# The last 512-column matmul of each second-product run, done as two matmuls of 256 columns

## The chip, the cores and the metric

The kernel runs on one core of a Trainium2 chip. The metric is the device time of one launch in microseconds, as the median of several runs. Five engines work side by side in a core: TensorE (PE in the rows; its weight loads are listed apart as PEld), VectorE (DVE), ScalarE (ACT), GpSimd (POOL) and SyncE (SP), which issues the DMAs.

## The reference

Three layers follow one another: attention with a memory term, a mixture of eight experts over 2304 tokens, and a two-matrix layer.

```python
def _moe_ref(x, w_gate, w1, w2):
    ...
    for e in range(E):
        h = np.maximum(x @ w1[e], 0.0)
        ye = h @ w2[e]
        out += P[:, e:e + 1] * ye

def _moe2_ref(x, w_in, w_out):
    h = x @ w_in
    g = np.maximum(0.01 * h, h)
    return g @ w_out
```

Tokens 2304, model width 512, eight experts of width 1024, then one layer of width 2048. All in float32; the kernel splits each operand into a high and a low part and multiplies three times (high by high, high by low, low by high).

## The kernel before

Attention and the first expert take the first fifth of the span. Everything after that is the main stage, the function `rest`: experts 1 to 7 and the last layer. Its order is written out by hand (manual scheduling); what stands in the code is what each engine does, in that order.

The main stage is a list of steps. A step is one block of tokens by 256 columns of the hidden width. There are four segments (line 749): 14 units by three token blocks, 14 by two, 4 by three, 4 by two, each times two halves (`fp`), which makes 84 + 56 + 24 + 16 = 180 steps. Blocks 0 and 1 of a segment have 512 tokens, block 2 has 256; so 144 steps have 512 tokens and 36 have 256.

A step has two products on TensorE:

- `l1` (line 781), the first product. For 512 tokens it is seven products (`PRODUCTS`, a Strassen-like scheme) of six matmuls each: 42 matmuls of 256 columns, all at line 810. For 256 tokens it is 24 matmuls of 256 columns, at line 798. The operands come in threes: weights high with x high, weights high with x low, weights low with x high.
- `l2` (line 841), the second product, into the PSUM banks `po[j]`, one for each 128 tokens. It is a run of 24 matmuls (12 for 256 tokens) of 512 columns, all at line 853: over two halves `f`, over `j`, and three operand pairs (`hh` with the high weights, `hh` with the low ones, `hl` with the high ones). Here a part of the hidden values (`hh`, `hl`) is the stationary operand, and the 512 columns of the second weight matrix stream through.

The loop of `rest` does `l1` of step k, and then `l2` of step k-1 (lines 962 and 965). So on TensorE a run of 42 or 24 matmuls of 256 columns and a run of 24 or 12 matmuls of 512 columns take turns, with two exceptions at the ends: two `l1` stand ahead of the first `l2`, and two `l2` stand at the end. In nine places eight transposes of 128 columns (line 915, which bring in the tokens of the next layer) stand between an `l2` and the next `l1`. Every matmul has its own weight load of 128 columns.

After the second half of a step (`fp` = 1), VectorE adds each `po[j]` to the accumulator `acc` (lines 861 to 867).

Of the kernel before, what the change touches and what calls it, by code (L numbers as in the profile page):

```python
# [20 lines left out]
P = 128  # L21
B, H, S, D = 4, 8, 576, 64
NT, DM, E, F, G = 2304, 512, 8, 1024, 2048
# [477 lines left out]
class First:  # L501
# [3 lines left out]
    T = 256  # L505
# [63 lines left out]
SB = 256  # L569
# [168 lines left out]
def rest(tc, pools, W, X, xd, Pm, ident, keep, out, conv):  # L738
# [3 lines left out]
    nc = tc.nc  # L742
# [16 lines left out]
    po, hs = {}, {}  # L759

    def tiles(st):

        seg, s = st[0], st[2]
        T = SB if s == 2 else 2 * SB
        return T, range(4 * s, 4 * s + T // P), seg["bases"][0] // P
# [75 lines left out]
    def l2(st):  # L841
        seg, u, s, fp, inst = st
        w = W.finish(inst)
        hh, hl = hs.pop(st[1:])
        T, ts, t0 = tiles(st)
        if fp == 0:
            for j in range(T // P):
                po[j] = pp.tile([P, DM], F32, tag=f"po{j}", name=f"po{j}")
        for f in range(2):
            for j in range(T // P):  # L850
                r = slice(j * P, (j + 1) * P)
                for n, (a, part) in enumerate(((hh, "h"), (hh, "l"), (hl, "h"))):
                    nc.tensor.matmul(po[j], a[:, f, r], w[1, part][:, f], start=(fp == 0 and f == 0 and n == 0), stop=(fp == 1 and f == 1 and n == 2))  # L853
        if last_of[inst] is st:
            W.gone.add((inst, 1))
        if fp == 0:
            return
        e = u // 2
        for j, t in enumerate(ts):
            if u == 2:  # L860
                nc.vector.tensor_scalar(out=acc[t], in0=acc[t], scalar1=Pm[:, t0 + t, 0:1], scalar2=None, op0=ALU.mult)
            if u < 16:
                nc.vector.scalar_tensor_tensor(out=acc[t], in0=po[j], scalar=Pm[:, t0 + t, e:e + 1], in1=acc[t], op0=ALU.mult, op1=ALU.add)  # L863
            elif u == 16:
                nc.scalar.activation(acc[t], po[j], AF.Copy)  # L865
            else:
                nc.vector.tensor_add(acc[t], po[j], acc[t])
            if u == 19:
                nc.sync.dma_start(out=out[(t0 + t) * P:(t0 + t + 1) * P, :], in_=acc[t])
# [84 lines left out]
    for k, st in enumerate(steps):  # L954
        seg, u, s, fp, inst = st
        if more is None or seg is not steps[k - 1][0]:
            assert more is None or next(more, None) is None
            more = side(seg["n"])
        for t in put_by:
            nc.sync.dma_start(out=keep[t * P:(t + 1) * P, :], in_=acc[t - seg_t0])  # L960
        put_by = []
        l1(st)
        if k:
            last = steps[k - 1]
            l2(last)
            if last[1] == 15 and last[3] == 1:
                _, ts, seg_t0 = tiles(last)
                put_by = [seg_t0 + t for t in ts]
        W.advance()
        next(more, None)  # L970
        if seg["n"] < 2:
            conv.advance(1 + (k % 2 if seg["n"] == 0 else 1))
    l2(steps[-1])
    assert next(more, None) is None and next(conv.todo, None) is None

# [174 lines left out]
```

## Time and profile before

| what | us |
|---|---|
| median of 3 runs | 2171.53 |
| lowest and highest | 2171.14, 2173.83 |
| the profiled execution, its own time | 2172.86 |
| the profiled execution, span from first to last instruction | 2171.1 |
| TensorE busy in the span | 2127.4 |
| VectorE busy in the span | 1384.9 |

The span is the time between the first and the last instruction of the profiled execution; 1.8 us of its own time lie around it. A matmul's busy time in the rows is longer than the distance to the next matmul, because matmuls overlap in the pipeline: what a matmul costs is read from the starts of neighbours in the timeline.

### The profile page before, as it was taken

What the parts mean: (1) busy time and instruction counts of PE and PEld (TensorE: products, weight loads), DVE (VectorE), ACT (ScalarE), POOL (GpSimd) and SP (SyncE); (2) the same over time, 40 slices, a digit from 0 to 9 for tenths busy, and PEclk for the clock granted to TensorE, in tenths of its full rate; (3) what the DMA queues carried; (4) which work ended last, traced back from release to release, by engine and by line L of the source; (5) the groups of instructions that cost most, each with busy time, mean ns of one, the idle gap of its engine ahead of it and who ended that gap; (6) DMA issues with size and microseconds to landing.
All of it is one profiled execution on the core that took longest, in us unless ns stands there. A gap on an engine that the chain in (4) does not pass through costs nothing.

```text
span 2171.1 us, 34909 instructions
## 1 busy us (share of the span) xinstructions
PE 2127.4 (98%) x13661; PEld 1878.7 (87%) x13661; DVE 1384.9 (64%) x2523; ACT 758.3 (35%) x1557; POOL 1082.2 (50%) x1007
## 2 busy tenths in 40 slices
PE   7999999999999999999999999999999999999999
PEld 4677777898899999999999889999999998898998
DVE  6666655367767777777766889655545453566565
ACT  6666652333322222222222233333232323333331
POOL 5322223447755544455445688745554444574540
PEclk8999999999999999999999999999999999999999
DMA  7433312245422221122226444311111152336111
GB/s 223 125 121 122 122 59 69 97 144 165 139 69 69 69 68 58 64 69 76 71 72 242 133 143 141 101 59 40 59 49 50 59 213 80 96 91 239 58 50 40
DMA packets 164582, 217.82 MB, mean 100 GB/s; under 512 B 14145, under 2 KB 109377, under 8 KB 162881
## 3 DMA queue, kind: packets, MB, share of 16 engines
q1 hardware_dynamic: 164416, 215.59, 30.5%
q8 instruction: 108, 1.77, 0.3%
q14 instruction: 58, 0.47, 0.1%
HBM read 166.23 MB, written 49.28 MB: 99 GB/s over the span
## 4 chain that ended last, share of the span: by engine, by line
PE 68%; DVE 5%; POOL 4%; issue 2%; DMA 2%; ACT 1%; POOLq 0%; DVEq 0%; SPq 0%; ACTq 0%
PE po L853 35%; PE pq L810 28%; PE pq L798 4%; PE po L493 1%; PE ph L485 1%; POOL w0l L600 1%; DMA raw<-in_moe_w_dram 1%; DVE hl L829 1%; POOL stl L658 1%; DMA xa<-xd 1%; POOL ql L600 0%; DVE c L820 0%; DVE c L831 0%; DVE acc L863 0%; POOL raw L614 0%
## 5 line engine op out<-in xcount | busy, mean ns | idle before, releaser
L853 PE MATMUL po<-w,hh 128*128 128x512 f32 x2592 | 799.0, 389 | 6.8 <-ACT acc L865 2.9
L853 PEld LDWEIGHTS po<-w,hh 128*128 128x128 f32 x2592 | 473.9, 188 | 95.9 <-ACT acc L865 3.1
L853 PE MATMUL po<-w,hl 128*128 128x512 f32 x1296 | 504.4, 389 | 0.0
L600 POOL TENSOR_TENSOR w0l<-raw,w0h 128x512 fp32r<-128x512 f32 x144 | 190.5, 1343 | 364.6 <-ACT w0h L599 364.6
L828 ACT ACTIVATE hh<-c 128x512 fp32r<-128x512 f32 x224 | 129.2, 624 | 482.3 <-DVE c L823 482.3
L853 PEld LDWEIGHTS po<-w,hl 128*128 128x128 f32 x1296 | 243.2, 188 | 50.7
L810 PE MATMUL pq<-Xh,w0h 128*128 128x256 f32 x960 | 270.8, 282 | 3.6 <-ACT xa L928 2.2
L810 PE MATMUL pq<-Xh,w0l 128*128 128x256 f32 x960 | 270.3, 282 | 0.0
L810 PE MATMUL pq<-Xl,w0h 128*128 128x256 f32 x960 | 270.3, 282 | 0.0
L829 DVE SCALAR_TENSOR_TENSOR hl<-c,hh 128x512 fp32r<-128x512 f32 x224 | 165.5, 780 | 79.1 <-ACT hh L828 79.1
L863 DVE SCALAR_TENSOR_TENSOR acc<-po,Pm,acc 128x512 f32<-128x512 f32 x252 | 176.0, 748 | 50.6 <-PE po L853 48.7
L600 POOL TENSOR_TENSOR w<-raw,w 128x512 fp32r<-128x512 f32 x144 | 197.6, 1390 | 0.9
L810 PEld LDWEIGHTS pq<-Xh,w0h 128*128 128x128 f32 x960 | 180.8, 188 | 8.0 <-ACT xa L928 2.4
L810 PEld LDWEIGHTS pq<-Xh,w0l 128*128 128x128 f32 x960 | 184.8, 192 | 0.0
L810 PEld LDWEIGHTS pq<-Xl,w0h 128*128 128x128 f32 x960 | 180.8, 188 | 3.5
L818 DVE TENSOR_TENSOR uv<-pq,s 128x256 f32<-128x256 f32 x144 | 60.4, 419 | 193.3 <-ACT s L817 193.2
L817 ACT ACTIVATE s<-pq 128x256 f32<-128x256 f32 x144 | 54.7, 380 | 257.9 <-PE pq L810 257.8
L600 POOL TENSOR_TENSOR ql<-raw,qh 128x512 fp32r<-128x512 f32 x48 | 62.6, 1325 | 134.1 <-ACT qh L599 134.1
L810 PE MATMUL pq<-Xh,w1h 128*128 128x256 f32 x384 | 107.9, 281 | 1.1 <-ACT xa L928 1.1
L810 PE MATMUL pq<-Xh,w1l 128*128 128x256 f32 x384 | 107.8, 281 | 0.0
L810 PE MATMUL pq<-Xl,w1h 128*128 128x256 f32 x384 | 107.8, 281 | 0.0
L810 PE MATMUL pq<-Xl,sh 128*128 128x256 f32 x384 | 107.8, 281 | 0.0
(257 smaller groups left out, 4847.1 us busy)
## 6 DMA issues: line engine op xcount, KB each, us to landing
raw<-in_moe_w_dram SPq DMA_DIRECT2D x136, 512.0 KB, 3.5
Xh<-kh SPq DMA_DIRECT2D x6, 1792.0 KB, 7.3
Xl<-kl SPq DMA_DIRECT2D x6, 1792.0 KB, 11.5
f<-in_moe_w_in_dram SPq DMA_DIRECT2D x16, 512.0 KB, 5.0
f<-in_moe_w_out_dram SPq DMA_DIRECT2D x16, 512.0 KB, 4.5
raw<-wide_in SPq DMA_DIRECT2D x16, 512.0 KB, 3.2
raw<-wide_out SPq DMA_DIRECT2D x16, 512.0 KB, 3.8
kh<-sth SPq DMA_DIRECT2D x12, 512.0 KB, 5.1
```

What stands on the lines that cost most here:

```text
L485: nc.tensor.matmul(ph[:, :T], wp[:, c, f0:f0 + P], x[:, c, t0:t0 + T], start=(n == 0), stop=(n == 11))
L493: nc.tensor.matmul(po, a[:, s], wp[:, c, :], start=(first and n == 0), stop=(last and n == 2))
L600: self.nc.gpsimd.tensor_sub(lo, src, f32(hi))
L658: sub(lo[:, m], r, f32(hi[:, m]))
L798: nc.tensor.matmul(ph[:, f * SB:(f + 1) * SB], wp(a, c % 2), xp[x][:, c], start=(n == 0), stop=(n == 11))
L810: nc.tensor.matmul(b[-1][:, o:o + SB], wp(a, c), X[s][part][:, x, c], start=(n == 0), stop=(n == 5))
L817: nc.scalar.activation(s1, b[0][:, lo], AF.Copy)
L818: v.tensor_add(uv[:, 0], b[0][:, up], s1)
L828: nc.scalar.activation(hh[:, f], c, AF.Relu)
L829: v.scalar_tensor_tensor(out=hl[:, f], in0=c, scalar=0.0, in1=f32(hh[:, f]), op0=ALU.max, op1=ALU.subtract)
L853: nc.tensor.matmul(po[j], a[:, f, r], w[1, part][:, f], start=(fp == 0 and f == 0 and n == 0), stop=(fp == 1 and f == 1 and n == 2))
L863: nc.vector.scalar_tensor_tensor(out=acc[t], in0=po[j], scalar=Pm[:, t0 + t, e:e + 1], in1=acc[t], op0=ALU.mult, op1=ALU.add)
```

## The change

In each `l2`, the very last matmul of the run (second half `f`, last token tile `j`, third operand pair: `hl` with the high weights) is written as two matmuls, one over columns 0 to 255 and one over columns 256 to 511 of the same bank, with the same stationary operand. The flag that ends the accumulation goes to the second of them. Nothing else is changed.

```diff
                 for n, (a, part) in enumerate(((hh, "h"), (hh, "l"), (hl, "h"))):
-                    nc.tensor.matmul(po[j], a[:, f, r], w[1, part][:, f], start=(fp == 0 and f == 0 and n == 0), stop=(fp == 1 and f == 1 and n == 2))
+                    for d in (slice(0, SB), slice(SB, DM)) if f and n == 2 and j == T // P - 1 else (slice(0, DM),):
+                        nc.tensor.matmul(po[j][:, d], a[:, f, r], w[1, part][:, f, d], start=(fp == 0 and f == 0 and n == 0), stop=(fp == 1 and f == 1 and n == 2 and d.stop == DM))
```

The order on TensorE where an `l2` ends and the next `l1` begins, before (`po_4884` is the bank of the last token tile, `x2` two alike):

```order
L853 MATMUL po_4884<-w_4234,hh 128x512 x2
L853 MATMUL po_4884<-w_4234,hl 128x512
L810 MATMUL pq<-Xh_3477,qh_3480 128x256
L810 MATMUL pq<-Xl_3478,qh_3480 128x256
L810 MATMUL pq<-Xh_3477,ql_3481 128x256
```

The same place in the changed kernel:

```order
L854 MATMUL po_4884<-w_4234,hh 128x512 x2
L854 MATMUL po_4884<-w_4234,hl 128x256 x2
L810 MATMUL pq<-Xh_3477,qh_3480 128x256
L810 MATMUL pq<-Xl_3478,qh_3480 128x256
L810 MATMUL pq<-Xh_3477,ql_3481 128x256
```

The row of one 512-column matmul has become a row of two with 256 columns, each with a weight load of its own; the unbroken chain of 256-column matmuls that follows is now 44 long (26 for 256 tokens) where it was 42 (24). No wait is added on any engine, and the other engines keep their order.

## Rows read from the trace of the kernel before

**Rows 1.** The page: span; busy times; line 853's group (count, busy us, mean ns, idle).

```profile
span 2171.1 us, 34909 instructions
PE 2127.4 (98%) x13661; PEld 1878.7 (87%) x13661; DVE 1384.9 (64%) x2523; ACT 758.3 (35%) x1557; POOL 1082.2 (50%) x1007
...
L853 PE MATMUL po<-w,hh 128*128 128x512 f32 x2592 | 799.0, 389 | 6.8 <-ACT acc L865 2.9
```

**Rows 2.** Two stretches: length, busy time by engine, clock, DMA; columns in first row.

```profile
core 0: us, PE busy (x) PEld busy (x) DVE busy (x) ACT busy (x) POOL busy (x), PEclk, DMA share, GB/s
458.30:463.79 5.49, 5.49 (x27) 4.51 (x25) 2.92 (x5) 3.03 (x6) 5.18 (x7) 1.00 0.05 17
468.74:474.18 5.44, 5.44 (x27) 4.50 (x26) 4.43 (x10) 1.01 (x2) 0.00 (x0) 1.00 0.83 281
```

**Rows 3.** TensorE's waits from 448 us on: total us, times, longest.

```profile
PE pq L810 <- ACT xa L928: 3.3, 2, 2.2
PE po L853 <- ACT acc L865: 2.9, 1, 2.9
PE po L853 <- DVE acc L863: 2.5, 5, 0.9
PE po L853 <- DVE acc L867: 1.3, 1, 1.3
PE pq L810 <- DVE uv L818: 1.2, 1, 1.2
```

**Rows 4.** TensorE's timeline through one step: start, us, engine, line, instruction.

```profile
463.79 0.28 PE L810 MATMUL pq<-Xh,qh 128*128 128x256 f32 x1
...
468.74 0.62 PE L853 MATMUL po<-w,hh 128*128 128x512 f32 x2
...
470.77 0.62 PE L853 MATMUL po<-w,hh 128*128 128x512 f32 x2
...
474.18 0.28 PE L810 MATMUL pq<-Xh,w0h 128*128 128x256 f32 x1
```

**Rows 5.** The same timeline in the first run of the second product.

```profile
458.30 0.63 PE L853 MATMUL po<-w,hh 128*128 128x512 f32 x2
458.77 0.40 PE L853 MATMUL po<-w,hl 128*128 128x512 f32 x1
459.01 0.62 PE L853 MATMUL po<-w,hh 128*128 128x512 f32 x2
...
460.39 0.61 PE L853 MATMUL po<-w,hh 128*128 128x512 f32 x2
```

**Rows 6.** Weight loads, 448.6 to 458.2 us, by operands: count, busy us, mean ns.

```profile
L810 PEld LDWEIGHTS pq<-Xh,w0h 128*128 128x128 f32 x14 | 2.7, 192 | 0.0
L810 PEld LDWEIGHTS pq<-Xh,w0l 128*128 128x128 f32 x14 | 2.6, 188 | 0.0
...
L853 PEld LDWEIGHTS po<-w,hh 128*128 128x128 f32 x1 | 0.2, 192 | 0.0
```

**Rows 7.** Weight loads of the next run, 463.8 to 468.7 us, same columns.

```profile
L810 PEld LDWEIGHTS pq<-Xh,sl 128*128 128x128 f32 x8 | 1.5, 192 | 0.0
...
L853 PEld LDWEIGHTS po<-w,hh 128*128 128x128 f32 x1 | 0.2, 187 | 0.0
```

**Rows 8.** TensorE's timeline in a run of 256 columns that follows transposes.

```profile
1225.05 0.28 PE L810 MATMUL pq<-Xh,qh 128*128 128x256 f32 x1
...
1229.47 0.63 PE L853 MATMUL po<-w,hh 128*128 128x512 f32 x2
...
1230.16 0.62 PE L853 MATMUL po<-w,hh 128*128 128x512 f32 x2
```

**Rows 9.** TensorE's timeline in the stage of the first expert, six matmuls apart.

```profile
442.51 0.39 PE L493 MATMUL po<-w1h,hh 128*128 128x512 f32 x1
...
443.89 0.28 PE L485 MATMUL ph<-xh,w0h 128*128 128x256 f32 x1
```

**Rows 10.** Half of the transposes: count, shortest, median, longest ns, first and last.

```profile
L915 PE MATMUL xt<-ident,ta x36: 272/273/273, 1223.8 to 1929.6; 128*128 128x128 f32 x36
```

## The prediction

> **What bounds the kernel now.** I read the busy shares first: TensorE is busy for 2127.4 of 2171.1 us, the next engine for 1384.9 [rows 1]. The list of TensorE's waits comes next. From 448 us to the end, which is the whole main stage, it waits for another engine some 11 us in all, in ten places [rows 3]. In the other 1700 us one matmul starts as soon as the one ahead of it lets it. The granted clock is 1.00, the upper of its two levels (2.4 GHz), in the stretches I looked at [rows 2]. So whatever the change adds on TensorE in the main stage is added to the end, and what it takes away there comes off; the other engines need not be followed, because they wait for TensorE and not the reverse. No wait is added and no queue is reordered: the second half of the split carries the signal to VectorE that the whole matmul carried.
>
> What is left is the price of one matmul after another, and that is read from starts. In a usual step the 42 matmuls of 256 columns take 468.74 - 463.79 = 4.95 us, 117.8 ns each; the 24 of 512 columns take 474.18 - 468.74 = 5.44 us, 226.7 ns each [rows 4]. Rows print hundredths of a microsecond, and the unrounded starts behind them give the same to a few tenths of a nanosecond.
>
> **Part 1, the split itself.** Two matmuls of 256 columns in place of one of 512 cost 2 x 117.8 - 226.7 = 8.9 ns if each costs what its kind costs in a usual step. There is one per step: 180 x 8.9 ns = 1.6 us. The lower bound for the pair is the cheapest 256-column matmul in the trace. In a run that follows transposes the fourth matmul starts at 1225.05 and the first 512-column one, 39 later, at 1229.47: 113.3 ns each [rows 8]. Two of these are 226.7, so the split would cost nothing. I take 8.9 ns, since the pair follows a run of 512 columns, as the usual 256-column runs do, and no transposes.
>
> The Trainium skill ("TensorE: Matmul & The Clock Gate", section "Back-to-back issue gap") gives the gap between warm matmuls as columns over 2.4 GHz plus 2.5 ns, by which the split would cost 2.5 ns, as an estimate 0.45 us for all 180. The trace differs: 256 columns more cost 108.9 ns, and the part that does not grow with the columns is 8.9 ns.
>
> **Part 2, where the 512-column run is entered.** The matmuls of the usual 256-column run repeat with a period of three. It shows in the weight loads: of each three, two take 188 ns and one 192 ns. In a usual run the long load belongs to the third operand pair (x high with weights low), so that after 42, a multiple of three, the first load of the 512-column run is a short one again, 187 ns [rows 7]. Such a run goes at 226.7 ns from its first matmul on. The 24-long chains of the 256-token steps are a multiple of three too.
>
> One run in the trace is entered elsewhere in this period: the first one, at 458.30. The chain ahead of it began after a wait, and its long load lies on the first operand pair (192 against 188), so that the long load also falls on the first matmul of the 512-column run, 192 ns [rows 6]. That run stumbles. Its first nine matmuls take 460.39 - 458.30 = 2.09 us [rows 5], where the nine of a usual run take 470.77 - 468.74 = 2.03 [rows 4]; the whole run takes 5.49 us against 5.44 [rows 2]. The unrounded starts of the two runs give 5.485 and 5.440, so 45 ns; after ten matmuls it is back at 226.7. DMA is not the reason: its share is 0.05 in the run that stumbles and 0.83 in the one that doesn't [rows 2].
>
> The changed kernel puts two matmuls of 256 columns ahead of the 42. If the period starts with the first 256-column matmul behind a 512-column run, as it does now, the chain is 44 (or 26) long, which leaves a remainder of two. The long load then falls on the third, sixth, ... of the chain, which is the first operand pair of the first product, and again on the first matmul of the 512-column run. That is just the place of the run at 458.30. So each run of the second product that is entered from such a chain should stumble by 45 ns, and since this takes ten matmuls, it fits into the 24 and also into the 11 full ones of a 256-token step; the next chain then starts afresh.
>
> How many are entered so: of 180 runs, the first is unchanged (no split ahead of it), nine stand behind a 256-column run that follows transposes (72 transposes, eight in a place [rows 10]) and keep their own start, and up to seven begin with a wait [rows 3]; that leaves 163. 163 x 45 ns = 7.3 us.
>
> **The sum.** 1.6 + 7.3 = 8.9 us. In the ten places where TensorE waits, the step's own 54 ns are partly hidden: at most 10 x 0.054 = 0.5 us off. I take 8.4 us. From the profiled execution's own time, 2172.86, that makes 2181.3; it lies 1.33 us above the median of the runs, 2171.53, so the median of the changed kernel should be 2179.9 us, 0.39% more. Bounds of the two terms: 0 to 8.9 ns for the split; for the stumble 0 (the usual entry) to 60 ns (the nine-matmul rows at the far end of their rounding); so 0 to 11 us.
>
> **Rivals.** *The entry stays in step.* The run at 458.30 is a single clean case of its kind, and it may be the wait ahead of that chain and not its place in the period that makes it stumble; or the pair, which reads the second weights and not x, does not start the period. Then only the split is paid: 1.5 us, 2173.0 us, no change that can be told. For it speaks that the usual runs show nothing at all, against it that the place of the long load is the one thing that sets the two entries apart. The stage of the first expert shows too that entries can differ without a wait: there six 512-column matmuls take 443.89 - 442.51 = 1.38 us, 20 ns over six usual ones [rows 9].
>
> *The pair puts the chain into the cheap state.* After the transposes the 256-column matmuls go at 113.3 ns for the whole run, with 15 ns or so lost at the entry of the 512-column run (three matmuls in 1230.16 - 1229.47 = 0.69 us where usual ones take 0.68) [rows 8]. If two matmuls of 256 columns from another product did what the transposes do, 135 chains of 42 and 34 of 24 would each win 4.5 ns a matmul: 6486 x 4.5 ns = 29 us, less 169 x 15 ns = 2.5 us, less the 1.6 us of the split: 25 us faster, 2147 us. Against it: the transposes have 128 columns, and behind every 512-column run the trace shows the 117.8 ns state, whichever weights and x follow.
>
> *Part of it.* The entry is off, but by an amount that no row shows (the third place of the period): between 0 and 45 ns, so 2173 to 2180.
>
> The rival on the far side of no change is thus the cheap state; it decides only if the second or third matmul behind the split starts 113 ns after its neighbour rather than 118.
>
> **How the numbers follow.** The forecast has 0.67, the entry in step 0.19, the cheap state 0.08, the partial entry 0.06, half of it above and half below the bound. A measurement of this kernel can tell about 0.2% (4.3 us) from no change. So faster 0.08, same 0.22, slower 0.70. The predicted time is the forecast's, 2179.9. The range leaves out the cheap state and the far ends: from 2172.0, which takes in the entry in step (2173.0 less 1 us of scatter between runs), to 2183.5, the upper bound of 11 us on the median with 1 us of scatter.
>
> **What would show it.** In the changed kernel's profile, 256-column rows at line 854 whose neighbours start 0.12 us apart (right for part 1), and 0.11 if the cheap state holds. The long weight load, 192 ns, on the first operand pair of line 810 instead of the third, and on the first load of line 854's run. The first nine 512-column matmuls of a usual run in 2.09 us, not 2.04, the mean duration of the matmuls at that line some nanoseconds above 389 [rows 1], and a run of 24 (23 full ones and the pair) in 5.49 + 0.01 us. If the long load sits there and the run does not stumble, the step from the period to the stumble is wrong; if the load stays on the third pair, the step from the pair to the period is.

## The result, and the profile after

| | before | after |
|---|---|---|
| median, us | 2172.41 (2171.14 to 2173.83, 4 runs) | 2151.75 (2151.47 to 2154.49, 4 runs) |
| ratio, with its 95% interval | | 0.9908 (0.9896 to 0.992) |
| span of the profiled execution, us | 2171.1 | 2149.7 |

The changed kernel is 0.9% faster, where 0.4% slower was forecast; the time lies outside the range. What came is the rival with a chance of 0.08, the cheap state. The page of the changed kernel (what answers to [rows 1]), with the groups of the two products: line, engine, operation, operands, count, then busy us, mean ns, idle time ahead.

```profile
span 2149.7 us, 35269 instructions
PE 2102.0 (98%) x13841; PEld 1858.8 (86%) x13841; DVE 1387.3 (65%) x2523; ACT 758.2 (35%) x1557; POOL 1082.9 (50%) x1007
...
L854 PE MATMUL po<-w,hh 128*128 128x512 f32 x2592 | 802.4, 391 | 9.3 <-DVE acc L864 4.3
...
L810 PE MATMUL pq<-Xh,w0h 128*128 128x256 f32 x960 | 266.7, 278 | 2.1 <-DVE uv L818 1.4
L810 PE MATMUL pq<-Xl,w0h 128*128 128x256 f32 x960 | 265.8, 277 | 0.0
```

180 matmuls more, as planned, and TensorE still busy to 98%, but 25 us less of it, 21 of them in the main stage. The matmuls of line 810 last 276 to 278 ns on average, where they lasted 281 to 282; those of the 512-column run 391 where they lasted 389. So the main stage's gain lies in the first product, which the diff doesn't touch. The timeline of TensorE in one step (columns as in [rows 4]):

```profile
707.11 0.62 PE L854 MATMUL po<-w,hh 128*128 128x512 f32 x2
707.56 0.40 PE L854 MATMUL po<-w,hl 128*128 128x256 f32 x2
707.80 0.29 PE L810 MATMUL pq<-Xh,w0h 128*128 128x256 f32 x1
707.92 0.28 PE L810 MATMUL pq<-Xl,w0h 128*128 128x256 f32 x1
708.04 0.28 PE L810 MATMUL pq<-Xh,w0l 128*128 128x256 f32 x1
708.15 0.28 PE L810 MATMUL pq<-Xh,w0h 128*128 128x256 f32 x1
708.27 0.28 PE L810 MATMUL pq<-Xl,w0h 128*128 128x256 f32 x1
...
712.58 0.63 PE L854 MATMUL po<-w,hh 128*128 128x512 f32 x2
...
713.27 0.62 PE L854 MATMUL po<-w,hh 128*128 128x512 f32 x2
```

From the fifth matmul of the chain, 708.27, to the first of the 512-column run, 712.58, 38 matmuls take 4.31 us: 113.4 ns each, against 117.8 in [rows 4]. The unrounded starts show the way in: the pair 114 and 119 ns, then 121, 122, 115, 115, and 113.3 from there on. The first three matmuls of the next 512-column run take 713.27 - 712.58 = 0.69 us, the small loss of [rows 8] and not the stumble of [rows 5]. The weight loads of this chain (708.2 to 712.5 us: count, busy us, mean ns) have no long one any more; against [rows 6, 7], all are short, and so is the first load of the 512-column run:

```profile
L810 PEld LDWEIGHTS pq<-Xh,w0h 128*128 128x128 f32 x13 | 2.4, 188 | 0.0
L810 PEld LDWEIGHTS pq<-Xh,w0l 128*128 128x128 f32 x13 | 2.4, 188 | 0.0
L810 PEld LDWEIGHTS pq<-Xl,w0h 128*128 128x128 f32 x13 | 2.4, 188 | 0.0
L854 PEld LDWEIGHTS po<-w,hh 128*128 128x128 f32 x1 | 0.2, 187 | 0.0
```

In the trace of the changed kernel all 169 chains that follow a split run directly are in this state; in the trace before, the 169 chains at the same places were in the other one. (The first two chains have no run ahead of them, and nine stand behind transposes; of these nine, all started in the cheap state before, and seven after: at 1344.38 and 1835.88 us the chain starts at 117.8 ns.)

### The profile page after: what moved, and what is told of

Read it like the earlier page. It is cut to its first block, busy times and chain, and to the rows that moved or that the text cites. A ratio compares the mean times of both kernels' runs of the same rounds, so it can differ in the third digit from the quotient of the medians.

```text
span 2149.7 us, 35269 instructions
## 1 busy us (share of the span) xinstructions
PE 2102.0 (98%) x13841; PEld 1858.8 (86%) x13841; DVE 1387.3 (65%) x2523; ACT 758.2 (35%) x1557; POOL 1082.9 (50%) x1007
## 4 chain that ended last, share of the span: by engine, by line
PE 74%; DVE 4%; POOL 2%; issue 2%; ACT 1%; DMA 0%; DVEq 0%; POOLq 0%; ACTq 0%
PE po L854 38%; PE pq L810 29%; PE pq L798 4%; PE po L493 1%; PE ph L485 1%; DVE hl L829 0%; POOL stl L658 0%; POOL ql L600 0%; DVE c L831 0%; DVE acc L864 0%; DMA raw<-in_moe_w_dram 0%; DVE c L820 0%; POOL w0l L600 0%; PE xt L916 0%; POOL raw L614 0%
## 5 line engine op out<-in xcount | busy, mean ns | idle before, releaser
L854 PE MATMUL po<-w,hl 128*128 128x512 f32 (+1 forms) x1476 | 507.0, 364 | 0.0
L854 PEld LDWEIGHTS po<-w,hl 128*128 128x128 f32 x1476 | 277.2, 188 | 58.5
L828 ACT ACTIVATE hh<-c 128x512 fp32r<-128x512 f32 x224 | 129.2, 624 | 478.2 <-DVE c L823 478.2
L810 PE MATMUL pq<-Xl,w0h 128*128 128x256 f32 x960 | 265.8, 277 | 0.0
L810 PE MATMUL pq<-Xh,w0l 128*128 128x256 f32 x960 | 265.4, 276 | 0.0
L829 DVE SCALAR_TENSOR_TENSOR hl<-c,hh 128x512 fp32r<-128x512 f32 x224 | 170.1, 800 | 79.1 <-ACT hh L828 79.1
L810 PEld LDWEIGHTS pq<-Xh,w0l 128*128 128x128 f32 x960 | 180.4, 188 | 0.0
L832 ACT ACTIVATE hh<-c 128x512 fp32r<-128x512 f32 x64 | 40.5, 632 | 186.6 <-DVE c L831 186.6
L810 PE MATMUL pq<-Xh,sh 128*128 128x256 f32 x384 | 106.2, 277 | 0.0
## 6 DMA issues: line engine op xcount, KB each, us to landing
Xl<-kl SPq DMA_DIRECT2D x6, 1792.0 KB, 11.4
```

The costliest lines, as they stand in the source:

```text
L810: nc.tensor.matmul(b[-1][:, o:o + SB], wp(a, c), X[s][part][:, x, c], start=(n == 0), stop=(n == 5))
L828: nc.scalar.activation(hh[:, f], c, AF.Relu)
L829: v.scalar_tensor_tensor(out=hl[:, f], in0=c, scalar=0.0, in1=f32(hh[:, f]), op0=ALU.max, op1=ALU.subtract)
L832: nc.scalar.activation(hh[:, f], c, AF.Copy)
L854: nc.tensor.matmul(po[j][:, d], a[:, f, r], w[1, part][:, f, d], start=(fp == 0 and f == 0 and n == 0), stop=(fp == 1 and f == 1 and n == ...
```

## The experiments

Words used below: a chain is the run of 42 (or 24) matmuls of the first product; it is cheap at 113.3 ns a matmul and dear at 117.8. The overcost of a step is the time from eleven 512-column matmuls ahead of a chain to ten behind its end, less 226.67 ns for every 512 columns in it, read from the starts in the trace. It takes in the split, the way in, the chain and the entry of the next run. Before, it is 187 ns for a chain of 42 (42 x 4.45); after, 40 ns (5 to 6 for the pair, 20 for the way in, 15 for the entry). Times without an interval are of one run; what is concluded from them rests on the traces, where the overcosts of like steps of one kernel agree within a few ns, and not on the last microsecond.

Theories at the start: N, the neighbour right ahead of the chain sets its state; S, the split acts on the program as a whole (its length, where its pieces lie); A, the addresses that load and stream read together; C, the count.

**Where the split stands, and what it reads: e1 to e4.** e1 splits the last but one matmul of the run, e2 takes the halves in the other order, e3 puts the last but one matmul between them, e4 splits all.

```diff
-todo = [(0, full), (1, full), (2, full)]
+todo = [(0, full), (1, lo), (1, hi), (2, full)] if end else ...     # e1
+todo = [(0, full), (1, full), (2, hi), (2, lo)] if end else ...     # e2
+todo = [(0, full), (2, lo), (1, full), (2, hi)] if end else ...     # e3
+todo = [(n, d) for n in range(3) for d in (lo, hi)]                 # e4
```

> The kernel before, with the last but one matmul of each run of the second product split into two of 256 columns, and the last one left at 512. Theory N (neighbour): what stands right ahead of the first product's chain sets its state; here that is a 512-column matmul again, so the chain goes at 117.8 ns a matmul as before, and the split costs 9 to 30 ns a step: 2172 to 2178 us. Theory S (somewhere): that the run holds a split at all, or that the program is longer by 180 matmuls, is what brings the cheap state: 113.3 ns and about 2152 us.

> The change, with the two halves in the other order (columns 256 to 511 first). If any two 256-column matmuls of the second product ahead of the chain do it (theory N alone): 113.3 ns a matmul in the chain, 2151 to 2153 us. If it hangs on which addresses the pair reads against each other (theory A, addresses): the state can change, 117.8 ns and 2173 to 2181 us.

> The same two halves, but the last but one 512-column matmul stands between them, so that a single 256-column matmul of the second product leads into the chain (43 long, remainder one of three). If the first 256-column matmul behind a 512-column one sets the state by what it reads (theory N): 113.3 ns, 2152 to 2156 us. If it takes two, or a chain of 44 (theory C, count): 117.8 ns and 2173 to 2183 us.

> Every matmul of the second product in the main stage as two of 256 columns, so that the main stage has no 512-column matmul and no change of length. If the cheap state holds wherever it is entered once: two at 113.3 ns cost what one 512-column matmul costs, and the 35 ns or so that each step pays at its two changes of length go: 2143 to 2148 us. If the second product's halves go at 117.8 ns: 24 x 9 ns a step more, about 2186 us, and about 2207 us if the first product's chain goes back to 117.8 ns with it.

Times: e1 2155.88, e2 2153.32, e3 2155.41, e4 2189.33 us, with 2169.9 for the kernel before on the same chip. In all four, all 169 chains are cheap. As e1's chain is 42 long and e3's 43, C falls, and in e2 swapping the halves changes nothing, so nothing there speaks for A. e1 speaks against N: a 512-column matmul stands right ahead of its chain again. But that matmul isn't a usual one: it takes 703.66 - 703.43 = 0.23 us, 233 ns unrounded, where a settled one takes 226.7, and the chain behind it takes a longer way in (117, 117, 118, 122, 118, 114 ns unrounded), which is why e1 is the slower. Timeline of e1:

```profile
703.43 0.40 PE L858 MATMUL po<-w,hl 128*128 128x512 f32 x1
703.66 0.28 PE L798 MATMUL pq<-xph,qh 128*128 128x256 f32 x1
...
704.37 0.28 PE L798 MATMUL pq<-xph,qh 128*128 128x256 f32 x1
704.48 0.28 PE L798 MATMUL pq<-xpl,qh 128*128 128x256 f32 x1
704.59 0.28 PE L798 MATMUL pq<-xph,ql 128*128 128x256 f32 x1
```

e4 lies near the middle number of its expectation, but by other terms: the first product is cheap (276 to 278 ns), while the second product's own 256-column matmuls settle at 120 ns each, worse than either state of the first product. The groups of e4 (count, busy us, mean ns, idle):

```profile
L858 PE MATMUL po<-w,hh 128*128 128x256 f32 x5184 | 831.7, 283 | 5.0 <-ACT acc L870 3.1 <-DVE acc L872 1.2 <-DVE acc L868 0.6
L858 PE MATMUL po<-w,hl 128*128 128x256 f32 x2592 | 522.6, 283 | 0.0
L810 PE MATMUL pq<-Xh,w0h 128*128 128x256 f32 x960 | 266.6, 278 | 1.8 <-DVE uv L818 1.2 <-ACT xa L933 0.5
```

So a fifth theory, P (phase): a settled run of 512-column matmuls hands over in one fixed timing of loads against matmuls, and that timing leads into the dear state; a run disturbed shortly before the handover does not.

**Place, dose, order, size: e5 to e8.**

```diff
-GAPS = {... "X0": 6, "X1": 0, ...}
+GAPS = {... "X0": 4, "X1": 2, ...}                                        # e5
-if f and n == 2 and j == T // P - 1 else
+if s == 0 and f and n == 2 and j == T // P - 1 else                       # e6
-for wp, part in ((wh, "h"), (wh, "l"), (wl, "h")):
+for wp, part in ((wl, "h"), (wh, "h"), (wh, "l")):                        # e7
+... (2, slice(0, P)), (2, slice(P, DM)) for the last matmul               # e8
```

> The kernel before, with the tiles of x for token block 0 moved by 512 bytes within each partition (gap units 6 to 4 ahead of them, 0 to 2 behind), the tiles of block 1 and all else left in place. Theory P (phase): the state of a chain is set by the timing at which a settled 512-column run hands over, not by where the operands lie, so all chains stay at 117.8 ns and the time at 2170 to 2174 us. Theory A (addresses): load and stream collide by where they read, so the chains of block 0 go at another pitch than those of block 1, in the same run: 113.3 or 120 ns against 117.8.

> The change in the steps of token block 0 alone (72 of 180). The split acts on the one chain behind it (both theories, since a 512-column run settles within its length): the chains behind block 0's runs, which are those of block 1, go at 113.3 ns, all others at 117.8; about 70 x 0.147 us = 10 us off, 2160 to 2163 us. If the split did something to the program as a whole (its length, where its pieces lie), all chains would be cheap (2152) or none (2172).

> The kernel before, with the three operand pairs of the first product in another order (weights low first, then high twice), and no split. Theory P: the chain is entered from a settled run as before, 117.8 ns, 2170 to 2174 us. Theory A: the first loads and streams read other places against each other at the handover, so the chain can land in the cheap state, 113.3 ns and 2145 to 2152 us.

> The change with unequal parts: 128 columns, then 384. The first part is shorter than its neighbour's weight load and costs about 109 ns instead of 57, so 50 ns a step (9 us) are lost in any case. Theory P: any disturbance of the settled run brings the cheap state, and 113.3 ns in the chain give 2158 to 2163 us. If it takes 256-column parts: 117.8 ns and 2179 to 2183 us.

(The move in e5 is 64 bytes, two units of eight floats, and not the 512 that its expectation says.) Times: 2179.46, 2160.91, 2172.36, 2161.74 us, before 2171.2.

e6 is the causal test, and it came as expected: 10 us off, and in one and the same run the chains behind split runs are cheap and those behind settled runs dear. Two chains of one unit in e6, the first behind a run without a split, the second behind one with:

```profile
761.42 0.28 PE L810 MATMUL pq<-Xh,qh 128*128 128x256 f32 x1
...
766.36 0.62 PE L854 MATMUL po<-w,hh 128*128 128x512 f32 x2
...
779.48 0.29 PE L810 MATMUL pq<-Xh,qh 128*128 128x256 f32 x1
...
784.26 0.63 PE L854 MATMUL po<-w,hh 128*128 128x512 f32 x2
```

42 matmuls in 4.94 us and in 4.78 us. In the whole trace it is 71 chains cheap and 98 dear. S falls with this. e7 changes what the chain's first loads and streams are and leaves all chains behind a settled run dear, as P says. e8's two parts take 57 and 229 ns (unrounded starts), 59 ns over one matmul of 512 columns where 50 were expected, and the loss shows at the second part and not at the first, as the expectation had it; every directly entered chain is still cheap.

e5 says that P is not all. Moving x of block 0 by 64 bytes, and nothing else, put the chains of block 0 at 119.9 ns on average (starts 117, 120 and 123 ns apart in turn), while those of block 1 stayed at 117.8, in the same run (first pair of rows: block 0, second: block 1):

```profile
764.85 0.28 PE L810 MATMUL pq<-Xh,qh 128*128 128x256 f32 x1
...
769.89 0.63 PE L853 MATMUL po<-w,hh 128*128 128x512 f32 x2
...
783.17 0.28 PE L810 MATMUL pq<-Xh,qh 128*128 128x256 f32 x1
...
788.12 0.39 PE L853 MATMUL po<-w,hh 128*128 128x512 f32 x1
```

5.04 us and 4.95 us. Which states there are thus hangs on where the operands lie; which of them a chain falls into, on the handover.

**The prediction's two steps apart, and more places: e9 to e12.** e9 lengthens each chain by two, with the chain's own operands; e10 to e12 move x of the three blocks by other amounts.

```diff
+if k == 0:                                                                # e9
+    for part in "hl":
+        nc.tensor.matmul(b[-1][:, o:o + SB], wh(a, 0), X[s][part][:, x, 0], start=True, stop=True)
-GAPS = {... "X0": 6, "X1": 0, "q": 10, ... "xp": 6, "h": 10}
+GAPS = {... "X0": 5, "X1": 2, "q": 9, ... "xp": 7, "h": 9}                # e10
+GAPS = {... "X0": 7, "X1": 1, "q": 8, ... "xp": 5, "h": 11}               # e11
+GAPS = {... "X0": 2, "X1": 3, "q": 11, ... "xp": 10, "h": 6}              # e12
```

> The kernel before with two more 256-column matmuls at the head of each chain of the first product, done with the chain's own first operands (into a bank that the chain then starts afresh, so that they add nothing to the output). It takes the prediction's two steps apart. They cost 2 x 117.8 ns a step, 42 us, in any case. If the step from a remainder of two to the stumble holds: chains at 117.8 ns, the long load on another operand pair, and 45 ns more at each entry of the 512-column run: 2220 to 2224 us. If a longer chain by itself brings the cheap state: 113.3 ns, about 2195 us. If neither: 2213 to 2216 us.

> The kernel before, with x moved within each partition: block 0 by -32 bytes, block 1 by +32, block 2 by +32; no split. Theory A+P (place and handover together): a settled run hands over into a state that the place of x against the weights sets, so each block gets a pitch of its own, one of 113.3, 117.8, 120 ns; a block at 113.3 gives 9 us back (72 chains of 42), at 120 it costs 8 us. Theory P alone: all at 117.8, 2170 to 2174 us.

> The same with block 0 by +32 bytes, block 1 by +64, block 2 by -32. Theory A+P: a pitch of its own for each block, 2150 to 2190 us by which they are; theory P alone: 117.8 ns throughout, 2170 to 2174 us.

> The same with block 0 by -128 bytes, block 1 by -32, block 2 by +128. Theory A+P: block 1 at the pitch that block 0 has in the run with -32, and a pitch of its own for -128 and +128; if 64 bytes are the width that counts, -128 changes nothing against before (117.8 ns). Theory P alone: 117.8 ns throughout, 2170 to 2174 us.

Times: 2217.73, 2180.62, 2181.99, 2177.25 us, before 2173.49. e9 does to the traces just what the prediction said of the change: the chains stay dear (168 of 169; the other begins behind a wait), the long load lies on the first operand pair and falls on the first matmul of the 512-column run, and that run stumbles, nine matmuls in 727.36 - 725.28 = 2.08 us (45 ns over settled ones, unrounded). Weight loads of e9 from 720.2 to 725.2 us, and the run behind them:

```profile
L816 PEld LDWEIGHTS pq<-Xh,w0h 128*128 128x128 f32 x14 | 2.7, 192 | 0.0
L816 PEld LDWEIGHTS pq<-Xl,w0h 128*128 128x128 f32 x14 | 2.6, 188 | 0.0
L816 PEld LDWEIGHTS pq<-Xh,w0l 128*128 128x128 f32 x14 | 2.6, 188 | 0.0
L859 PEld LDWEIGHTS po<-w,hh 128*128 128x128 f32 x1 | 0.2, 192 | 0.0
```

```profile
725.28 0.63 PE L859 MATMUL po<-w,hh 128*128 128x512 f32 x2
...
727.36 0.62 PE L859 MATMUL po<-w,hh 128*128 128x512 f32 x2
```

Its time is 44.2 us over that of before, and the terms give 42.4 + 7.4 = 49.8. TensorE's waits in it are 6.8 us where they were 11.4, which accounts for 4.6 of the difference: a slower TensorE waits less for the others.

e10 to e12 (mean over the chain, in ns a matmul, behind a settled run, by how far x was moved):

| bytes | -128 | -64 | -32 | 0 | +32 | +64 |
|---|---|---|---|---|---|---|
| blocks 0 and 1 | 117.9 | 119.9 | 118.7 | 117.8 | 118.4 | 119.8 |

The mean for -32 came out at 118.7 in block 0 (e10) and in block 1 (e12) alike; for block 2, +32 gave 118.3, -32 118.9, +128 117.9. The pitch goes by place, so theory P alone falls; and at none of the places tried is a settled handover cheap, so none of them can replace the split.

**Which handovers are cheap: e13 and e14.** Two kernels in which each unit of the first two segments rearranges the tail of its second product in its own way, 28 ways each.

```diff
+ops = [(f, j, n, 0, DM) for f in range(2) for j in range(T // P) for n in range(3)]
+ops = arranged(ops, seg["n"], u, s)      # one way for each unit: cut(ops, back, at), half_ahead(ops), ...
```

> One kernel in which each unit of the first two segments treats the last matmuls of its second product in its own way (28 ways: no split; one split of 256/256 at the last, last but one, ... up to the ninth from the end; unequal splits of the last one, 128 to 384 columns; two and three splits; halves interleaved; another order of the last three, with a split and without). Since a 512-column run settles within its length, the ways do not touch one another, and each is read from its own chains. Theory P at this place of x: every way that leaves the run unsettled when it hands over (a split in the last ten matmuls) gives 113.3 ns in the chain, the ways without a split 117.8 ns; they differ in what the split and the way to the cheap state cost, 25 to 80 ns a step. If the handover must hit the state by chance, about half of the unsettled ways stay at 117.8 ns. Whole time 2152 to 2165 us, without meaning.

> A second kernel of this kind: 28 further ways, finer cuts of the last matmul (260 to 304 columns first), unequal cuts of the last but one and the one before, a half ahead with unequal parts, and a cut of 272/240 at the end together with a cut at the head of the run; the last two segments use 272/240 throughout. If the handover meets the cheap state by its timing, ways that differ by 4 to 8 columns (2 to 3 ns) can differ in state, and some 15 to 20 of the 28 are cheap; the cheapest way in costs between 0 and 33 ns a step over the bare columns (the pair: 40; 272/240: 33). If the cheap state were a matter of the kind of split and not of the timing, the cuts from 260 to 304 would all behave alike. Whole time 2150 to 2165 us, without meaning.

Whole times 2168.18 and 2165.46 us. Overcost of a step in ns, chains of 42, by way:

| way | cheap | dear |
|---|---|---|
| no split, two ways | | 187, 187 |
| last matmul cut at column | 128: 100, 256: 40, 260: 33, 262: 47, 264: 47, 272: 33, 274: 47, 276: 47, 288: 53, 296: 47, 384: 94 | 192: 260, 224: 247, 240: 240, 248: 194, 268: 213, 270: 240, 280: 220, 304: 206, 320: 213 |
| cut at 256, how many matmuls from the end | 0: 40, 1: 53, 2: 53, 4: 53 | 3: 253 (one chain of four cheap), 5: 220, 6: 220, 8: 220 |
| last but one cut at | 208: 74, 224: 47, 256: 53 | 192: 220, 216: 207, 240: 200, 248: 193, 272: 240, 288: 247, 320: 260 |

This rules out the kind of split as the cause. A cut at 268 or 270 columns is dear, at 264 or 272 it is cheap: steps of 2 to 4 columns, which at 226.67 ns for 512 are 1 to 2 ns. Two neighbouring units of e14, cut at 270 and at 274, each chain from its start to the next run:

```profile
1416.52 0.28 PE L848 MATMUL pq<-Xh,w0h 128*128 128x256 f32 x1
...
1421.47 0.39 PE L893 MATMUL po<-w,hh 128*128 128x512 f32 x1
```

```profile
1458.29 0.28 PE L848 MATMUL pq<-Xh,w0h 128*128 128x256 f32 x1
...
1463.07 0.63 PE L893 MATMUL po<-w,hh 128*128 128x512 f32 x2
```

4.95 us and 4.78 us. So it is not any disturbance that does it (16 of the 26 ways with a split in e13 are cheap), and e13's stronger expectation falls; which state the chain falls into is met or missed by a nanosecond. A split of the fifth matmul from the end (4 in the table) still brings the cheap state; those further ahead leave the dear one, and their price is paid all the same.

The same traces show what the long load's place goes by. Behind every cut of the last matmul the two parts and the chain of 42 make the same count, 44, and yet these chains fall into four states, not two (loads and entries unrounded, all chains of 42 that no wait disturbs):

| last matmul cut at | long load on | the next 512-column run loses |
|---|---|---|
| 192, 224, 240, 270 | first operand pair | 45 ns |
| 268, 280 | second operand pair | 22 ns |
| 248, 304, 320 | third operand pair, as before | 0 ns |
| the other eleven | none (cheap) | 15 ns |

Loads of one chain each and the first load of the run behind it, cut at 270 (e14, 1416.6 to 1421.4 us), at 268 (e14, 571.3 to 576.1) and at 248 (e13, 1664.1 to 1668.9):

```profile
L848 PEld LDWEIGHTS pq<-Xh,w1h 128*128 128x128 f32 x8 | 1.5, 192 | 0.0
...
L893 PEld LDWEIGHTS po<-w,hh 128*128 128x128 f32 x1 | 0.2, 193 | 0.0
```

```profile
L848 PEld LDWEIGHTS pq<-Xl,w0h 128*128 128x128 f32 x14 | 2.7, 192 | 0.0
...
L893 PEld LDWEIGHTS po<-w,hh 128*128 128x128 f32 x1 | 0.2, 188 | 0.0
```

```profile
L844 PEld LDWEIGHTS pq<-Xh,w1l 128*128 128x128 f32 x8 | 1.5, 192 | 0.0
...
L889 PEld LDWEIGHTS po<-w,hh 128*128 128x128 f32 x1 | 0.2, 188 | 0.0
```

So the handover picks the place of the long load as well as the pitch. With the cut at 240 or 270 columns, all that the prediction forecast of the change comes about: 53 ns over the usual step, where it had 54.

**The best way in every step: e15 and e16.**

```diff
-for d in (slice(0, SB), slice(SB, DM)) if
+for d in (slice(0, 272), slice(272, DM)) if                               # e15; e16 is the changed kernel
```

> The change with the cut at 272 instead of 256 columns, in every step. If what the scans read from single chains adds up over the kernel: chains at 113.3 ns, and a way in that costs 33 ns instead of 40 over the bare columns, so 170 x 7 ns = 1.2 us under the changed kernel: 2150 to 2151.5 us, 0.99 of the kernel before. If the scans' steps had helped each other, some chains would fall back to 117.8 ns and the time would lie above 2152 us.

> The changed kernel itself, timed beside the one with 272/240 on the same chip: 2151 to 2153 us, 0.990 to 0.992 of the kernel before.

e15 2153.34 us, ratio 0.9914 (0.99 to 0.9928); e16 2153.9 us, ratio 0.9915 (0.9901 to 0.9929); before 2171.5 on the same chip. Both beat the kernel before; the 1.2 us between 33 and 40 ns a step can't be told from their scatter of 4 to 6 us. Both lie above what was expected, but no chain fell back because of the cut: e15's trace has all 169 directly entered chains cheap, at 33 to 34 ns a step where e16's has 40.

In e16 one of the 169 is dear, the one at 1822.74, and it tells timing from place. The kernel is the changed one, so the same chain stands in the first trace, at 1819.77: same instructions, same operands in the same places, both begun behind a wait of TensorE (idle 1.44 us there, 1.42 in e16). From the second matmul to the 39th, first in the trace of the changed kernel, then in e16:

```profile
1819.99 0.28 PE L810 MATMUL pq<-Xl,w0h 128*128 128x256 f32 x1
...
1824.20 0.28 PE L810 MATMUL pq<-Xh,w0l 128*128 128x256 f32 x1
```

```profile
1822.96 0.28 PE L810 MATMUL pq<-Xl,w0h 128*128 128x256 f32 x1
...
1827.32 0.28 PE L810 MATMUL pq<-Xh,w0l 128*128 128x256 f32 x1
```

4.21 us and 4.36 us, 113.8 ns (with the way in) and 117.8. The instructions, their order and the places are the same in both; when things happened is what can differ.

## Why the prediction was wrong, point by point

**What bounds the kernel** was right: TensorE alone counted, its waits in the main stage were 11.4 us before and add up to 12.9 after, and what changed on TensorE came to the end. Of the 21.4 us between the spans 1.4 lie ahead of the main stage, whose first matmul starts at 448.3 us before and at 446.9 after, and are not the change's. The 20.0 of the main stage, by overcosts: 135 chains of 42 at 147 ns and 34 of 24 at 67 ns are 22.1 us; the two chains at the start, which came out cheap too, 0.4; longer waits, -1.5; chains behind transposes, -0.4: 20.6 us.

**Part 1, the split**, was about right: the pair costs 5 to 6 ns over a 512-column matmul (232 to 233 against 226.7), where 8.9 was taken and 0 to 8.9 given. The gap that the prediction takes there from the Trainium skill ("TensorE: Matmul & The Clock Gate", section "Back-to-back issue gap") is given on that page for an isolated matmul; these stand in an unbroken stream, so the difference in the trace does not contradict it, and no run here shows an isolated one.

**Part 2 holds the step that failed.** Its text hangs on "if the period starts with the first 256-column matmul behind a 512-column run", so that the count of 44 gives the place of the long load. The pair does not start the period: its second half follows after 113 to 114 ns, the chain's first matmul after 119 more, and from its fifth matmul the chain goes at 113.3 ns with no long load at all. In place of 7.3 us for stumbles of 45 ns the 512-column runs lose 15 ns each, and the steps give 22.1 us back with split, way in and entry paid. The cuts of e13 and e14 show that the count was never what sets the place: with 44 in every one, the long load comes to lie on the first, second or third operand pair or nowhere, by where the cut is. What the prediction made of the place holds: where the long load falls on the first operand pair, the run stumbles by 45 ns, with two matmuls of the chain's own (e9) as with a pair cut at 240 or 270. So the case at 458.30 was read rightly, and the step from the pair to the period was wrong. That the cut at 256 meets the cheap state, and not the one forecast, is a matter of a few nanoseconds (at 248 and at 268 columns the chain is dear), and no row of the trace before shows which way it falls.

**The rivals.** The cheap state was named with its mechanism, and priced at 25 us where its chains gave 22.1: the way in, 20 ns a step or 3.4 us, was left out, and the pair was taken some 0.6 us too dear. Its test was half right: the second half of the pair did follow after 113 ns, but the state held only from the fifth matmul of the chain. What was badly off is its chance. The trace before has settled handovers, which are all dear, and nine others behind transposes, all cheap (one until a wait broke it off). The change makes a handover that is not settled, so the nine were the cases to count; e13 puts such handovers at 16 in 26 and e14 at 17 in 28, and behind transposes, too, two of nine came out dear in the changed kernel, though the prediction had these keep their own start. The forecast weighed the one clean case at 458.30, a chain of its own operands alone, over these nine. *Part of it* had the third place of the period between 0 and 45 ns: it is 22 ns (cuts at 268 and 280).

**Shown and not shown.** Shown: the state is chosen at each handover (e6), not by the kind of split (e13, e14) nor by the count of matmuls, and it can differ where instructions, operands and places are the same (e16 against the changed kernel); steps of 1 to 2 ns in the cut change it. The set of pitches goes by the operands' place (e5, e10 to e12). The cuts move the place where the second part starts along with the timing, so that timing alone sets the state in them too is argued from the pair of traces and not shown cut by cut. Also not shown: why a load takes longer in the dear state. Loads start some 3 to 4 ns behind the matmul ahead in both states, and the matmul follows its own load by 110 ns in the cheap and 114 to 115 in the dear one (unrounded starts). It is not the clock: the granted clock is 1.00 in the stretches of [rows 2] and in a cheap chain of the changed kernel (start and end, length, busy time of each engine, clock, DMA share, GB/s):

```profile
707.80:712.60 4.80, 4.80 (x45) 4.80 (x44) 4.59 (x6) 1.02 (x2) 4.80 (x4) 1.00 0.38 113
```

Each trace has one stretch of 3.4 us at a granted clock of 0.5, the lower level, in the main stage, behind a long wait of TensorE (from 1856.9 us before, from 1828.6 after); as it stands in both, it doesn't make the difference.

The Trainium skill ("TensorE: Matmul & The Clock Gate", section "LDWEIGHTS (loading the stationary operand)") has a load take its columns over 1.2 GHz; for 128 columns that is, as an estimate, 107 ns, which is also 256 columns at 2.4 GHz. By that rule a chain of 256 columns would be the length at which loads have nothing to spare. The traces neither confirm nor refute it: from a load's start to its matmul's start it is 110 to 115 ns in chains of 256, near that estimate, but the load's own row lasts 187 to 192 ns; in runs of 512 it is 223 to 224 ns, and no state but one shows there. That this is the reason, no run here tests.

## What to carry to other kernels

Where matmuls run back to back, each with a weight load of its own, look at starts in the timeline, not at busy shares (98% before and after here): a chain can have steady pitches some per cent apart, here 113.3 and 117.8 ns, and a change of one instruction ahead of it can move it from one to another. When a change alters such a handover, count the cases in the trace by whether they were settled, and give an unsettled handover odds near even between cheap and dear instead of carrying over one case; here 33 of 54 ways came out cheap. To search such a thing, try many ways in one run: where each step forgets the last, every unit can have its own variant, and one trace compares 28 of them.

## What the runs showed of the hardware that was not expected

- The same chain of 256-column matmuls has steady pitches of 113.3, 117.8 and, with x 64 bytes aside, 119.9 ns on average; a chain keeps its state to its end unless a wait breaks it.
- At 117.8 ns every third load is long (192 ns against 188), and what the next 512-column run loses goes by which operand pair has it: 45, 22 or 0 ns; at 113.3 ns no load is long and the run loses 15 ns (e13, e14).
- The same chain of the same kernel, begun behind a wait, went at 113.3 ns in one execution and at 117.8 in another (1819.77 us in the changed kernel's trace, 1822.74 in e16's).
- 2 columns in the cut of one 512-column matmul (270 against 272, or 262 against 260 in the way in) change the state of the 42 matmuls behind it or the price of reaching it by 14 to 207 ns.
- After a chain of 256 columns a run of 512 takes up to ten matmuls and 45 ns to come back to 226.7 ns, and from the cheap state three matmuls and 15 ns.
- The second product's own operands, cut to 256 columns, settle at 120 ns (e4).
